# Attention and feed-forward on one core: VectorE's share of the exponentials chosen while scheduling, late groups added from another bank

## Chip, cores, metric

One core of a Trainium2 chip. The time is device time in microseconds (us), the median over executions; lower is better.

## The reference

```python
x = A_x                                             # [1, 2048, 512] bf16
g = sigmoid((x * gate_w).sum(-1, keepdims=True))
a = mha(x, wqkv, wo)                                # 32 heads of 16, softmax over 2048 keys
b = (silu(x @ w_gate) * (x @ w_up)) @ w_down        # 512 -> 1792 -> 512
return g * a + (1 - g) * b
```

Attention has 32 × 2048 × 2048 = 134 million exponentials. They are most of ScalarE's work: 841.0 of its 864.7 busy us.

## The kernel before

The work is cut into 32 units (four heads, 512 queries). A unit has 64 banks of scores, each 128 keys by 512 queries for one head. A bank goes one of two ways:

- two banks at a time through ScalarE (`s_t` to `e_t`, one exponential instruction of 128x1024);
- one bank at a time through VectorE (`d_t` to `y_t`): an eviction that scales the score so that its 16-bit pattern is nearly the exponential, and after four banks (a *block*) seven more steps of 128x2048 that correct it.

Either result is multiplied by V into `o_ps`, the only output bank. At the end of a unit `o_ps` is copied out. PSUM's eight banks are all taken: four for `s_t`, one each for `d_t` and `o_ps`, two (`m`) shared by projections and the feed-forward part.

The order of instructions is fixed while building by a small planner that keeps a reckoned time for TensorE, VectorE and ScalarE. Cut to what matters here:

```python
def on_vector(b):            # VectorE's banks: eight fixed places in each unit but the first
    return b % (4 * KT) in (0, 7, 14, 21, 32, 39, 46, 53) and 4 * KT <= b < 4 * (SLOTS - KT) + 24

def emit_pair(bs):           # two banks for ScalarE
    ...
    act(out=e_t[:], in_=s_t[:], func=ACT.Exp, scale=inv_sqrt_dh)
    plan.act = max(plan.act, plan.pe + 0.27) + 0.905

def first():                 # in emit_d: one bank for VectorE
    vec.tensor_scalar(out=y[:, i * QBW:(i + 1) * QBW], in0=d_t[:, :], scalar1=EXP_A, scalar2=EXP_B, ...)
    ...                      # after the fourth: seven steps are queued in vops, 0.73 or 1.26 us reckoned each;
                             # the last one appends the block to `late`
def pv(bs):                  # multiply by V; a unit's one output bank
    ...
    mm(o_of[un][32 * j:32 * j + 32, :], lhsT=vaug[...], rhs=e_of.pop(b), start=(i == 1), stop=(i == KT), ...)

def emit_pv():
    ...
    if complete(closed):     # only when all 64 banks, late blocks too, are in
        close(closed); closed += 1
```

## Time and profile before

| | before |
|---|---|
| time | 900.39 us (900.07 to 900.48, 4 runs) |
| ScalarE busy | 864.7 us, 96% |
| exponential instructions on ScalarE | 902 |
| VectorE busy; its blocks | 738.3 us, 82%; 61 |
| ScalarE's wait for scores | 10.9 us in 16 waits |
| TensorE's wait for ScalarE to free a score buffer | 74.6 us |

An engine that is busy for 96% of the span and waits for 10.9 us in it is the bound. How the lines show this is in the prediction below. One view also belongs here: the granted TensorE clock (PEclk, the column after the engines; 1.00 is the full clock) around ScalarE's longest gap, in steps of 3.4 us.

```profile
core 0: us, PE busy (x) PEld busy (x) DVE busy (x) ACT busy (x) POOL busy (x), PEclk, DMA share, GB/s
86.10:89.50 3.40, 3.40 (x11) 0.57 (x10) 2.63 (x3) 3.26 (x4) 0.00 (x0) 0.57 0.02 5
89.50:92.90 3.40, 1.55 (x13) 0.53 (x11) 2.18 (x4) 2.07 (x3) 0.00 (x0) 0.93 0.33 74
92.90:96.30 3.40, 3.40 (x18) 0.49 (x15) 3.16 (x5) 2.05 (x2) 0.00 (x0) 0.50 0.00 1
96.30:99.70 3.40, 3.40 (x25) 0.74 (x22) 0.81 (x2) 1.74 (x2) 0.00 (x0) 0.56 0.02 5
```

From 89.5 to 92.9 us TensorE is busy for only 1.55 of 3.4 us, since it waits for the late block and the copy. In the 6.8 us that follow it is granted about half its clock, and ScalarE is busy for 3.8 of them: to the gap of 2.33 us come two waits of 0.92 us. So the unit-end wait is paid twice here.

### The profile page before, as it was taken

The numbers are of one execution on the slowest core, as the hardware profiler recorded it, in microseconds if no ns is written. First come the engines' busy times: TensorE is split into PE (matmuls) and PEld (weight loads), VectorE is DVE, ScalarE is ACT, GpSimd is POOL, SyncE is SP. The second block draws the span as 40 slices with busy tenths as digits, with TensorE's granted clock in tenths as the row PEclk, the third lists the DMA queues.
The fourth block names the chain that finished last, engine by engine and source line by source line (L and its number), as shares of the span: only waits on it lengthen the run. The fifth ranks groups of instructions, "written<-read, shape, count | busy, mean of one in ns | idle before, by whom it ended". The sixth has DMA issues, their size and how long they took to land.

```text
span 899.6 us, 14223 instructions
## 1 busy us (share of the span) xinstructions
PE 800.7 (89%) x5168; PEld 207.8 (23%) x5168; DVE 738.3 (82%) x1032; ACT 864.7 (96%) x967; POOL 7.0 (1%) x29
## 2 busy tenths in 40 slices
PE   6999899999998899999889888989888889888886
PEld 2222222222222222222222222222222222222221
DVE  6379898998988889887878889978787988887784
ACT  3999899999999999999999999999999999999996
POOL 3000000000000000000000000000000000000000
PEclk9999899999999999999999999999999999999999
DMA  8301021121101112110001111100011121000000
GB/s 205 105 1 32 22 48 33 38 54 27 34 7 28 36 36 68 37 48 10 5 15 40 33 51 48 52 15 10 4 25 34 35 54 46 21 10 5 6 19 24
DMA packets 87534, 31.97 MB, mean 36 GB/s; under 512 B 75120, under 2 KB 87016, under 8 KB 87464
## 3 DMA queue, kind: packets, MB, share of 16 engines
q1 hardware_dynamic: 86408, 30.94, 14.0%
q8 instruction: 40, 0.66, 0.3%
q10 hardware_dynamic: 1056, 0.13, 0.1%
q14 instruction: 30, 0.25, 0.1%
HBM read 20.83 MB, written 2.34 MB: 26 GB/s over the span
## 4 chain that ended last, share of the span: by engine, by line
ACT 44%; PE 32%; issue 11%; DVE 10%; SPq 1%; DMA 1%; ACTq 0%; DVEq 0%
ACT e_t L161 41%; PE s_t L158 12%; PE o_ps L158 7%; DVE y_t L167 4%; DVE u_t L167 3%; ACT th L161 3%; PE gp L158 3%; PE d_t L158 2%; PE up L158 2%; PE dps L158 2%; PE kp L158 1%; PE a_ps L158 1%; SPq L174 1%; PE qp L158 1%; DVE mt L167 1%
## 5 line engine op out<-in xcount | busy, mean ns | idle before, releaser
L161 ACT ACTIVATE e_t<-s_t 128x1024 bf16<-128x1024 f32 x902 | 841.0, 1075 | 11.6 <-PE s_t L158 10.9
L158 PE MATMUL s_t<-qx,kaug 64*128 64x512 bf16 x1692 | 330.9, 385 | 74.3 <-ACT e_t L161 72.8
L167 DVE TENSOR_SCALAR y_t<-d_t 128x512 uint16<-128x512 f32 x244 | 167.7, 687 | 85.1 <-PE d_t L158 81.6
L158 PEld LDWEIGHTS <-kaug 64*128 64x128 bf16 x2048 | 101.6, 93 | 404.3 <-issue 397.7
L158 PE MATMUL o_ps<-e_t,vaug 128*32 128x512 bf16 x1804 | 172.5, 391 | 1.6 <-DVE osb L167 0.8
L167 DVE TENSOR_TENSOR u_t<-u_t,z_t 128x2048 f16<-128x2048 f16 x122 | 148.9, 1220 | 2.4
L158 PE MATMUL d_t<-qx,kaug 64*128 64x512 bf16 x228 | 85.7, 376 | 0.0
L167 DVE TENSOR_TENSOR y_t<-y_t,u_t 128x2048 uint16<-128x2048 uint16 x61 | 74.3, 1218 | 0.6
L158 PEld LDWEIGHTS <-vaug 128*32 128x32 bf16 x2048 | 44.1, 95 | 132.7 <-issue 129.0
L158 PE MATMUL gp<-xT,wg 128*128 128x512 bf16 x224 | 68.5, 388 | 0.0
L158 PE MATMUL dps<-wd_t,mt 128*128 128x512 bf16 x224 | 67.8, 384 | 0.0
L158 PE MATMUL up<-xT,wu 128*128 128x512 bf16 x224 | 67.1, 387 | 0.0
L167 DVE SCALAR_TENSOR_TENSOR gs<-th,gp 128x512 bf16<-128x512 bf16 x56 | 38.2, 681 | 15.2 <-ACT th L161 14.8
L167 DVE TENSOR_SCALAR u_t<-z_t 128x2048 f16<-128x2048 uint16 x61 | 42.2, 692 | 1.6
L167 DVE TENSOR_SCALAR z_t<-y_t 128x2048 uint16<-128x2048 uint16 x61 | 42.2, 691 | 1.6
L167 DVE TENSOR_SCALAR u_t<-u_t 128x2048 f16<-128x2048 f16 x61 | 41.9, 686 | 0.8
L167 DVE SCALAR_TENSOR_TENSOR mt<-gs,up 128x512 bf16<-128x512 bf16 x56 | 38.2, 682 | 5.0 <-PE up L158 4.0
L167 DVE TENSOR_SCALAR y_t<-y_t 128x2048 uint16<-128x2048 uint16 x61 | 41.7, 684 | 0.3
L161 ACT ACTIVATE th<-gp 128x512 bf16<-128x512 f32 x56 | 36.2, 647 | 0.0
L158 PE MATMUL o_ps<-y_t,vaug 128*32 128x512 bf16 x244 | 24.6, 390 | 4.8 <-DVE y_t L167 4.7
L167 DVE CAST osb<-o_ps 128x512 bf16<-128x512 f32 x32 | 21.9, 685 | 7.6 <-PE o_ps L158 7.4
L158 PEld LDWEIGHTS <-mt 128*128 128x128 bf16 x263 | 16.3, 99 | 45.9 <-issue 38.8
(97 smaller groups left out, 316.1 us busy)
## 6 DMA issues: line engine op xcount, KB each, us to landing
wg<-in_B_w_gate_dram SPq DMA_DIRECT2D x56, 128.0 KB
wu<-in_B_w_up_dram SPq DMA_DIRECT2D x56, 128.0 KB
on<-osb SPq DMA_DIRECT2D x120, 16.0 KB
rb<-rr SPq DMA_DIRECT2D x15, 128.0 KB
wd_t<-in_B_w_down_dram SPq DMA_DIRECT2D x1, 1792.0 KB
qx<-qst SPq DMA_DIRECT2D x112, 16.0 KB
out_dram<-o_t SPq DMA_DIRECT2D x12, 128.0 KB
kaug<-on SPq DMA_DIRECT2D x20, 64.0 KB
```

The lines of the kernel that those rows point to most:

```text
L158: ordered(nc.tensor.matmul(*args, **kw))
L161: ordered(nc.scalar.activation(*args, **kw))
L167: return lambda *a, **kw: ordered(f(*a, **kw))
L174: nc.sync.dma_start_transpose(out=xT[:, dc, :], in_=x[:, dc * P:(dc + 1) * P])
```

## The change

The intent is to give VectorE an exponential whenever the planner finds it free, not at fixed places, and to let a unit close without its late blocks. A block that is late (a *late group*) is multiplied into one of the two `m` banks. VectorE then adds that bank to the unit's copied output (`of`, fp32). A unit closes after its sixteenth row of four banks, late blocks or not (`last`). To make room, the kernel has 12 buffers of exponentials in place of 15, and three `y` buffers for two.

```diff
-    EB = 15
+    EB = 12
-    def on_vector(b):
-        return b % (4 * KT) in (0, 7, 14, 21, 32, 39, 46, 53) and 4 * KT <= b < 4 * (SLOTS - KT) + 24
+    vset = set()
 ...
     def pv(bs, last):
         un = bs[0] // (4 * KT)
+        extra = un < closed
+        if extra:
+            o = m_tile("x_ps")
 ...
+        if extra:
+            def add():
+                blocks[un] -= 1
+                vec.tensor_tensor(out=(of_of if blocks[un] else osbs)[un][:, :], in0=of_of[un][:, :], in1=o[:, :],
+                                  op=ALU.add)
+                m_free(plan.dve)
+                if not blocks[un]:
+                    finish(un)
+            later(0.6, add)
 ...
-        vec.tensor_copy(out=osb[:, :], in_=o_of.pop(un)[:, :])
+        if blocks.get(un):
+            of_of[un] = work.tile([P, QBW], F32, tag="of", name="of", bufs=1)
+        vec.tensor_copy(out=(of_of if blocks.get(un) else osbs)[un][:, :], in_=o_of.pop(un)[:, :])
 ...
-        if complete(closed):
+        if last:
             close(closed)
 ...
-        if ... 0.216 * mms + (0.1 if plan.mode != "F" else 0.0) > most:
+        if ... 0.226 * mms + (0.1 if plan.mode != "F" else 0.0) > most:
 ...
+    def to_vector():
+        un, at_ = divmod(nxt, 4 * KT)
+        if vcur:
+            if nxt % 4 in [b % 4 for b in vcur["b"]]:
+                return 0
+            return 2 if at_ >= 4 * KT - 4 * (NV - vcur["i"]) else 1
+        if not un or at_ > (50 if un < UNITS - 1 else 4) or y_live[0] >= 3 or sum(v[0] for v in vops) > 6:
+            return 0
+        return 1
```

More of the change, by code (lines that the diff above doesn't have):

```diff
@@ L648, in emit_d @@
             y_live[0] += 1
-            vcur["y"] = vex.tile([P, NV * QBW], U16, tag="y", name="y_t", bufs=2)
+            blocks[b // (4 * KT)] = blocks.get(b // (4 * KT), 0) + 1
+            vcur["y"] = vex.tile([P, NV * QBW], U16, tag="y", name="y_t", bufs=3)
             vcur["i"], vcur["b"] = 0, []
@@ L667, in first @@
             mine = list(block["b"])
-            assert sorted(m % 4 for m in mine) == list(range(4))
+            assert sorted(m % 4 for m in mine) == list(range(4)) and mine[0] // (4 * KT) == mine[-1] // (4 * KT)
             vops.extend([
@@ L711, with pv @@
     o_of = {}
-    pv_n = {}
+    begun = set()
+    of_of = {}
+    blocks = {}
+    closed = 0
     o_end = [0.0]
-    def pv(bs):
+    def pv(bs, last):
         un = bs[0] // (4 * KT)
-        if un not in o_of:
-            while un and un - 1 not in osbs:
-                pay()
-            plan.pe = max(plan.pe, o_end[0])
-            o_of[un] = ps_o.tile([P, QBW], F32, tag="o", name="o_ps")
+        extra = un < closed
+        if extra:
+            o = m_tile("x_ps")
+        else:
+            if un not in o_of:
+                while un and un - 1 not in osbs:
+                    pay()
+                plan.pe = max(plan.pe, o_end[0])
+                o_of[un] = ps_o.tile([P, QBW], F32, tag="o", name="o_ps")
+            o = o_of[un]
         for b in bs:
             n, j = b // 4, HEADS[b % 4]
-            i = pv_n[un, j] = pv_n.get((un, j), 0) + 1
+            first = extra or (un, j) not in begun
+            begun.add((un, j))
             c0 = (4 * UNIT[un][1] + j) * VC
@@ L728, in pv @@
                 force(v_chain[n])
-            mm(o_of[un][32 * j:32 * j + 32, :], lhsT=vaug[:, n % KT, c0:c0 + 32], rhs=e_of.pop(b),
-               start=(i == 1), stop=(i == KT), tile_position=(0, 32 * j), skip_group_check=True)
+            mm(o[32 * j:32 * j + 32, :], lhsT=vaug[:, n % KT, c0:c0 + 32], rhs=e_of.pop(b),
+               start=first, stop=extra or last, tile_position=(0, 32 * j), skip_group_check=True)
             e_left.pop(b, None)
         spend("C", 1, max(e_end.pop(b, 0.0) for b in bs))
-    def complete(un):
-        return all(pv_n.get((un, j)) == KT for j in range(4))
+        if extra:
[7 more added lines that the diff above has]
+            later(0.6, add)
     onc = {}
@@ L753, in post, with settle @@
         osbs[un] = osb
-        vec.tensor_copy(out=osb[:, :], in_=o_of.pop(un)[:, :])
+        if blocks.get(un):
+            of_of[un] = work.tile([P, QBW], F32, tag="of", name="of", bufs=1)
+        vec.tensor_copy(out=(of_of if blocks.get(un) else osbs)[un][:, :], in_=o_of.pop(un)[:, :])
+    def settle(un):
+        qb, g = UNIT[un]
+        osb = osbs[un]
         if g == 1:
@@ L957, with finish, part @@
     nb = 4 * SLOTS
-    a_banks = [b for b in range(nb) if not on_vector(b)]
-    pq = [a_banks[i:i + 2] for i in range(0, len(a_banks), 2)]
-    dq = [b for b in range(nb) if on_vector(b)]
+    nxt = 0
     done = 0
-    closed = 0
     here = {}
+    def finish(un):
+        settle(un)
+        qb, g = UNIT[un]
+        if qb < QB - 1 and g == G - 1:
+            recip(qb, G, plan.slot)
+        if qb == QB - 1 and g == G - 3:
+            recip(qb, G - 2, plan.slot)
+        if un == UNITS - 2:
+            here[un] = recip_here(osbs[un])
+            spend("F", 1, plan.dve + 0.2)
+            for i in range(TQ):
+                def part(cs=slice(i * P, (i + 1) * P)):
+                    recip16(here[un][1][:, cs], here[un][0][:, cs])
+                    vec.tensor_tensor(out=osbs[un][:, cs], in0=osbs[un][:, cs], in1=here[un][1][:, cs],
+                                      op=ALU.mult)
+                    if cs.stop == QBW:
+                        m_free(plan.dve)
+                later(1.2, part)
     def close(un):
@@ L968, in f @@
             o_end[0] = plan.dve + 0.1
-            qb, g = UNIT[un]
-            if qb < QB - 1 and g == G - 1:
-                recip(qb, G, plan.slot)
-            if qb == QB - 1 and g == G - 3:
-                recip(qb, G - 2, plan.slot)
-            if un == UNITS - 2:
-                here[un] = recip_here(osbs[un])
-                spend("F", 1, plan.dve + 0.2)
-                for i in range(TQ):
-                    def part(cs=slice(i * P, (i + 1) * P)):
-                        recip16(here[un][1][:, cs], here[un][0][:, cs])
-                        vec.tensor_tensor(out=osbs[un][:, cs], in0=osbs[un][:, cs], in1=here[un][1][:, cs],
-                                          op=ALU.mult)
-                        if cs.stop == QBW:
-                            m_free(plan.dve)
-                    later(1.2, part)
+            if not blocks.get(un):
+                finish(un)
         later(0.6, f)
     def pv_ready(now):
-        if late and late[0][1][0] // (4 * KT) == closed and (now is None or late[0][0] <= now):
-            return late[0][1]
+        if late and (now is None or late[0][0] <= now):
+            un = late[0][1][0] // (4 * KT)
+            if un == closed or un < closed and (now is None or m_ready() is not None and m_ready() <= now):
+                return late[0][1]
         if done < SLOTS and done // KT == closed and not (now is not None and done in v_chain
                                                           and not v_chain[done].done()):
-            bs = [b for b in range(4 * done, 4 * done + 4) if not on_vector(b)]
+            bs = [b for b in range(4 * done, 4 * done + 4) if b not in vset]
             if all(b in e_of for b in bs) and (now is None or max(e_end[b] for b in bs) <= now):
@@ L999, in pvs_ready @@
     def pvs_ready(now):
-        if pv_ready(now) is None:
-            return 0
-        if late and late[0][1][0] // (4 * KT) == closed and late[0][0] <= now:
-            n = done
-        else:
-            n = done + 1
-        if len(late) > 1 and late[1][0] <= now and late[1][1][0] // (4 * KT) == closed:
-            return 2
-        if n < SLOTS and n // KT == closed and not (n in v_chain and not v_chain[n].done()):
-            bs = [b for b in range(4 * n, 4 * n + 4) if not on_vector(b)]
-            if all(b in e_of for b in bs) and max(e_end[b] for b in bs) <= now:
-                return 2
-        return 1
+        k = n = 0
+        for ready, bs in late[:2]:
+            un = bs[0] // (4 * KT)
+            if ready <= now and (un == closed or un < closed and k == 0 and m_ready() is not None and m_ready() <= now):
+                k += 1
+        for n in (done, done + 1):
+            if n < SLOTS and n // KT == closed and not (n in v_chain and not v_chain[n].done()):
+                bs = [b for b in range(4 * n, 4 * n + 4) if b not in vset]
+                if all(b in e_of for b in bs) and max(e_end[b] for b in bs) <= now and (
+                        closed in o_of or (not closed or closed - 1 in osbs) and o_end[0] <= now):
+                    k += 1
+        return min(k, 2)
     def emit_pv():
@@ L1017, in emit_pv @@
         bs = pv_ready(None)
-        pv(bs)
-        if late and late[0][1] is bs:
+        is_late = late and late[0][1] is bs
+        last = not is_late and done % KT == KT - 1
+        pv(bs, last)
+        if is_late:
             late.pop(0)
             y_live[0] -= 1
+            if bs[0] // (4 * KT) == closed:
+                blocks[closed] -= 1
         else:
             done += 1
-        if complete(closed):
+        if last:
             close(closed)
@@ L1044, in side @@
         t = m_ready() if takes else 0.0
-        if t is None or t > plan.pe + 0.1 or 0.216 * mms + (0.1 if plan.mode != "F" else 0.0) > most:
+        if t is None or t > plan.pe + 0.1 or 0.226 * mms + (0.1 if plan.mode != "F" else 0.0) > most:
             return None
@@ L1054 @@
     SLACK = 0.2
-    while pq:
-        if pq[0][-1] // 4 > plan.slot:
+    def to_vector():
[7 more added lines that the diff above has]
+        return 1
+    while nxt < nb:
+        if min(nxt + 1, nb - 1) // 4 > plan.slot:
             begin(plan.slot + 1)
@@ L1068 @@
         if room > 0.02:
-            d_ok = (vcur or y_live[0] < 2) and dq and dq[0] <= pq[0][-1] + 2 and not d_wait and d_end[0] <= plan.pe + 0.05
-            if d_ok:
-                emit_d(dq.pop(0))
+            if to_vector() and not d_wait and d_end[0] <= plan.pe + 0.05:
+                vset.add(nxt)
+                emit_d(nxt)
+                nxt += 1
                 continue
@@ L1086 @@
                 continue
-        if dq and dq[0] + 6 <= pq[0][0]:
-            while not vcur and y_live[0] >= 2:
-                next_pv()
-            emit_d(dq.pop(0))
+        if to_vector() == 2:
+            vset.add(nxt)
+            emit_d(nxt)
+            nxt += 1
             continue
-        emit_pair(pq.pop(0))
-    while closed < UNITS:
+        emit_pair(list(range(nxt, min(nxt + 2, nb))))
+        nxt += 2
+    while closed < UNITS or late or vops:
         fill_dve()
@@ L1103 @@
         else:
-            while pv_ready(None) is None:
-                pay()
-            emit_pv()
+            next_pv()
     for c in sorted(pace.chains, key=lambda c: c.deadline):
@@ L1115 @@
         pay()
-    assert not vops and not late and not dq and not d_wait
+    assert not vops and not late and not vcur and not d_wait and nxt == nb
     assert not at
```

## The prediction

> **What bounds the kernel now.** I read the page first: busy share by engine, then the costliest groups.
>
> ```profile
> PE 800.7 (89%) x5168; PEld 207.8 (23%) x5168; DVE 738.3 (82%) x1032; ACT 864.7 (96%) x967; POOL 7.0 (1%) x29
> ...
> L161 ACT ACTIVATE e_t<-s_t 128x1024 bf16<-128x1024 f32 x902 | 841.0, 1075 | 11.6 <-PE s_t L158 10.9
> L158 PE MATMUL s_t<-qx,kaug 64*128 64x512 bf16 x1692 | 330.9, 385 | 74.3 <-ACT e_t L161 72.8
> L167 DVE TENSOR_SCALAR y_t<-d_t 128x512 uint16<-128x512 f32 x244 | 167.7, 687 | 85.1 <-PE d_t L158 81.6
> ```
>
> ScalarE is busy for 96% of the span. Its 902 exponentials of two score banks each waited only 11.6 us in all, while the score matmuls waited 74.3 us, nearly all of it for ScalarE to free a score buffer. VectorE makes the other exponentials, 244 banks in 61 blocks of four, and waits 81.6 us for TensorE to deliver them. So ScalarE is the bound; the other two engines have about 75 and 160 us to spare. The mean of 1075 ns counts overlap twice. The step comes from the timeline of ScalarE: 71 exponentials in one run of 65.32 us, 0.920 us each, and 22 in 20.32 us, 0.924. I use 0.923.
>
> Next, the same by stage, to see whether this holds everywhere:
>
> ```profile
> core 0: us, PE busy (x) PEld busy (x) DVE busy (x) ACT busy (x) POOL busy (x), PEclk, DMA share, GB/s
> 20.00:60.00 40.00, 36.66 (x216) 9.79 (x214) 18.48 (x28) 38.48 (x43) 0.00 (x0) 1.00 0.25 67
> 60.00:150.00 90.00, 84.64 (x555) 22.04 (x557) 81.64 (x116) 85.45 (x96) 0.00 (x0) 0.94 0.15 32
> 150.00:400.00 250.00, 232.02 (x1506) 59.88 (x1505) 218.82 (x300) 248.11 (x281) 0.00 (x0) 0.99 0.16 38
> 400.00:640.00 240.00, 215.64 (x1412) 54.70 (x1413) 198.54 (x266) 238.66 (x266) 0.00 (x0) 1.00 0.11 27
> 640.00:870.00 230.00, 200.12 (x1308) 51.14 (x1301) 189.95 (x257) 229.18 (x257) 0.00 (x0) 1.00 0.10 25
> ```
>
> From 150 us on ScalarE leaves about 4 us of 720 idle. Only the stage from 60 to 150 us, where the projections of keys and queries fall, has three engines near 91 to 95% and ScalarE idle for 4.5 us. The timeline there shows why:
>
> ```profile
> 90.82 0.69 DVE L167 TENSOR_SCALAR y_t<-y_t 128x2048 uint16<-128x2048 uint16 x1
> 91.56 0.40 PE L158 MATMUL o_ps<-y_t,vaug 128*32 128x512 bf16 x4 [1.06 <-DVE y_t L167]
> ...
> 92.01 0.69 DVE L167 CAST osb<-o_ps 128x512 bf16<-128x512 f32 x1 [0.50 <-PE o_ps L158]
> ...
> 92.76 0.62 PE L158 MATMUL o_ps<-e_t,vaug 128*32 128x512 bf16 x3 [0.79 <-DVE osb L167]
> ...
> 94.01 2.11 ACT L161 ACTIVATE e_t<-s_t 128x1024 bf16<-128x1024 f32 x2 [2.33 <-PE s_t L158]
> ```
>
> A unit (64 score banks) cannot close until its last VectorE block is done (90.82), multiplied by V (91.56) and copied out of the only output bank (92.01); TensorE stands still in between, and ScalarE runs dry for 2.33 us. This is the place that the second half of the change is about. It is rare: over the whole trace the output matmuls waited 4.7 us for late blocks, in 10 waits.
>
> **What the Trainium skill says.** "ScalarE: Activation LUTs", section "What ACT_TABLE_LOAD costs", gives 186 ns plus 0.833 ns per element with immediate operands, and about 93 ns of overlap back to back: 946 ns for 1024 elements. The trace's step of 920 ns is 3% less; I use the trace's. "VectorE: DVE Perf Modes", section "Why PSUM operands drop a tier", holds fp32 from PSUM to one element per cycle. The trace agrees: 512 elements from PSUM take 687 ns, as long as 2048 16-bit elements from SBUF (z_t<-y_t, 691 ns). So the new adds, which read a PSUM bank, will not be cheap. "TensorEngine Tiling (Array Packing)", section "Key Properties", says that changing the tiling mode drains TensorE. The timeline agrees: from a lone score matmul (d_t, 308.49) to the next output matmul (308.79) is 0.30 us, where a step in one mode is about 0.21, so a change costs some 0.09 us.
>
> **The change, part by part.** I counted instructions in the two built orders.
>
> ScalarE: 902 exponentials become 890; the share of VectorE goes from 61 to 67 blocks. The six extra blocks lie in units 8, 14, 17, 22, 26 and 29, all in the stretch where ScalarE is the bound, so the saving is on the path: 12 × 0.923 = 11.1 us.
>
> VectorE: a block is four evictions of 687 ns, four cheap steps of 692, 691, 686 and 684, and three products or sums of 1220, 1220 and 1218: 9.16 us. Six of them: 55.0 us. New are 31 adds of a late group (output bank copy plus the other bank). No such row exists yet; the nearest is kaug<-a_ps,gval,bblk, one PSUM and one SBUF operand, at 749 ns: 31 × 0.749 = 23.2 us, an estimate. The copies out of the output bank stay 32 (28 of them now to fp32; 685 ns assumed for both). Together +78.2 us. All rows of VectorE add up to about 772 us against 738.3 busy, since neighbours overlap, so I scale by 0.956: +75 us, 813 us busy, some 91% of the new span.
>
> TensorE: the number of matmuls is the same, 5168. But 12 pairs, which run side by side in the two row halves, become 24 single scores: 12 more steps of 0.21, 2.5 us. Mode changes go from 1543 to 1573: 30 × 0.09 = 2.7 us. Against 74.3 us of waiting for ScalarE, 5 us of TensorE are covered.
>
> Waits: the unit-end chain shown above goes away, as a late group now uses one of the two banks shared with the projections and the feed-forward part, and no longer holds the output bank. I put this at 3 us (the 2.33 us gap and a few tenths elsewhere). Fewer buffers for exponentials (12 for 15) should not matter then, as they bridged just this wait.
>
> Sum: 900.36 − 11.1 − 3 = 886.3, before anything that a fuller VectorE costs.
>
> **The rivals.** First, VectorE becomes the bound. For units 6 to 30 I multiplied the changed order by the rows' durations: VectorE 673 us, 644 after scaling; ScalarE needs 688 × 0.923 = 635 plus 48 tanh at about 0.48 = 658. (The tanh figure: from first to last exponential 870.5 us, less 11 idle, less 902 × 0.923, over 56.) That is 98%, against 85% before; in units 14 to 22 it is 235 against 234. Such a full engine is sometimes late, and there is one bank for VectorE's scores and there are two buffers for ScalarE's, so TensorE waiting 1 us for VectorE makes ScalarE wait too. For it: these ratios. Against it: the schedule reckons 0.73 and 1.26 us for steps that take 0.69 and 1.22, and 0.905 us for an exponential that takes 0.923, so on the chip VectorE will tend to be ahead of the order it was given. I expect some 4 us; if late VectorE work struck at each of the six fuller units and some of the others, 10 to 15 us, and the time would be 896 to 901.
>
> Second, the late groups take the shared bank from the projections, which need two in turn, and each add stands in front of other VectorE work. In the stage from 60 to 150 us nothing is gained (no exponential leaves it), while 4 to 5 adds come in where VectorE is at 91%. If it costs 1 us per late group in that stage and a few tenths later, it takes back 5 to 10 us: 892 to 897. For it: the three full engines there. Against it: the planner puts a late group down only when such a bank is free.
>
> Third, better than reckoned: all of ScalarE's 11.6 us of waits go away as well. That is the floor, 900.36 − 11.1 − 11.6 = 877.7, and unlikely, as 1.5 us lie before VectorE has any share, and another 1.5 us at 872 to 875 us, where a matmul of the last step needs a just finished unit.
>
> **Range and chances.** 886.3 plus 4 for VectorE's lateness gives 890. Down to 884 if that costs nothing and the first stage gets smoother; up to 898 if VectorE is late at most fuller units. Over 2% faster means below 882.4 us, which needs nearly all of ScalarE's waits gone: 6%. Over 2% slower means above 918.4 us, 30 us of new ScalarE idle time: 2%.
>
> **What would show it.** Right: 890 exponentials with a step still near 0.923; ScalarE busy near 854 us; its wait for scores between 8 and 18 us; VectorE near 813 us, its wait for d_t well below 81.6, near 30; score matmuls waiting for ScalarE 55 to 70 us; output matmuls waiting for VectorE's blocks or the copy near zero, none above 1 us. Wrong: ScalarE waits of over 20 us, with TensorE waiting for VectorE (scores for d_t, or the shared bank) just before; adds much dearer than 0.75 us; or a lower granted TensorE clock over a long stretch, which the order of instructions cannot tell.

## The result, and the profile after

The changed kernel takes **885.19 us** (884.99 to 886.99, 4 runs), 0.9836 of the time before, 95% interval 0.9819 to 0.9853. Ratios here are the mean time of one kernel's fast runs over that of the other's of the same rounds, so not quite the ratio of the medians that are quoted. The time lies inside the stated range (884 to 898), near its fast edge; 10.4 us less were forecast, and 15.2 us came.

The page of the changed kernel, busy shares and the rows that answer to those shown before; the last row is the new add:

```profile
PE 784.8 (89%) x5078; PEld 207.2 (23%) x5168; DVE 797.8 (90%) x1129; ACT 853.5 (97%) x955; POOL 7.0 (1%) x29
...
L160 ACT ACTIVATE e_t<-s_t 128x1024 bf16<-128x1024 f32 x890 | 830.3, 1080 | 7.0 <-PE s_t L157 6.0
L157 PE MATMUL s_t<-qx,kaug 64*128 64x512 bf16 x1668 | 333.3, 385 | 59.9 <-ACT e_t L160 55.8
L166 DVE TENSOR_SCALAR y_t<-d_t 128x512 uint16<-128x512 f32 x268 | 184.0, 687 | 28.0 <-PE d_t L157 25.1
...
L166 DVE TENSOR_TENSOR osb<-of,x_ps 128x512 bf16<-128x512 f32 x28 | 19.1, 681 | 2.8 <-PE x_ps L157 2.7
```

ScalarE is still the bound. It works 11.2 us less (864.7 to 853.5), and waits for scores 4.9 us less (10.9 to 6.0). With 0.5 us from an earlier first exponential (19.8 for 20.3 us) that is 16.6, against 16.3 by which the span fell (899.6 to 883.3). VectorE has 75.8 us less idle time (59.5 us more work in a span 16.3 us shorter); 56.5 us of it are its wait for scores, which went from 81.6 to 25.1 us. (TensorE's busy time is of 5078 matmul records, 90 are missing, so it isn't compared.)

By stage, the changed kernel:

```profile
core 0: us, PE busy (x) PEld busy (x) DVE busy (x) ACT busy (x) POOL busy (x), PEclk, DMA share, GB/s
60.00:150.00 90.00, 84.25 (x585) 23.65 (x593) 85.55 (x122) 90.00 (x103) 0.00 (x0) 1.00 0.15 33
...
400.00:640.00 240.00, 217.38 (x1403) 55.29 (x1421) 223.44 (x306) 237.98 (x267) 0.00 (x0) 1.00 0.10 27
```

The stage from 60 to 150 us gained most: ScalarE, idle there for 4.55 us before, is never idle, and the granted clock is 1.00 for 0.94. From 400 to 640 us ScalarE has slightly more idle time than before, 2.0 for 1.3 us. The longest wait of the changed kernel comes later, at 737 us, and looks like the first rival of the prediction:

```profile
734.81 0.39 PE L157 MATMUL d_t<-qx,kaug 64*128 64x512 bf16 x1
...
735.05 1.22 DVE L166 TENSOR_TENSOR u_t<-u_t,z_t 128x2048 f16<-128x2048 f16 x1
...
736.19 0.68 DVE L166 TENSOR_SCALAR y_t<-d_t 128x512 uint16<-128x512 f32 x1
736.79 0.74 DVE L166 SCALAR_TENSOR_TENSOR o_t<-a_ps,gval,bblk 128x512 bf16<-128x512 f32 x1
...
736.93 0.37 PE L157 MATMUL d_t<-qx,kaug 64*128 64x512 bf16 x1 [0.98 <-DVE y_t L166]
...
737.62 1.02 ACT L160 ACTIVATE e_t<-s_t 128x1024 bf16<-128x1024 f32 x1 [1.08 <-PE s_t L157]
```

VectorE evicts `d_t` late (736.19), since its order has a step of 1.22 us in front (735.05). TensorE, which wants to write the next bank there, stands for 0.98 us, and ScalarE runs dry for 1.08 us. Whether VectorE is late because it is full, or because of that order alone, e7 will tell.

### The profile page after: what moved, and what is told of

Read it like the earlier page. It is cut to its first block, busy times and chain, and to the rows that moved or that the text cites. A ratio compares the mean times of both kernels' runs of the same rounds, so it can differ in the third digit from the quotient of the medians.

```text
span 883.3 us, 14242 instructions
## 1 busy us (share of the span) xinstructions
PE 784.8 (89%) x5078; PEld 207.2 (23%) x5168; DVE 797.8 (90%) x1129; ACT 853.5 (97%) x955; POOL 7.0 (1%) x29
## 4 chain that ended last, share of the span: by engine, by line
ACT 40%; PE 29%; DVE 17%; issue 10%; SPq 1%; DMA 1%; DVEq 0%; ACTq 0%
ACT e_t L160 37%; PE s_t L157 11%; DVE y_t L166 7%; PE o_ps L157 6%; DVE u_t L166 5%; ACT th L160 3%; PE d_t L157 3%; PE dps L157 2%; PE gp L157 2%; PE qp L157 1%; PE up L157 1%; SPq L173 1%; DVE mt L166 1%; PE kp L157 1%; DVE gs L166 1%
## 5 line engine op out<-in xcount | busy, mean ns | idle before, releaser
L160 ACT ACTIVATE e_t<-s_t 128x1024 bf16<-128x1024 f32 x890 | 830.3, 1080 | 7.0 <-PE s_t L157 6.0
L166 DVE TENSOR_SCALAR y_t<-d_t 128x512 uint16<-128x512 f32 x268 | 184.0, 687 | 28.0 <-PE d_t L157 25.1
L166 DVE TENSOR_TENSOR u_t<-u_t,z_t 128x2048 f16<-128x2048 f16 x134 | 163.4, 1219 | 1.9
L157 PE MATMUL d_t<-qx,kaug 64*128 64x512 bf16 x252 | 95.0, 377 | 1.7 <-DVE y_t L166 1.3
L166 DVE TENSOR_TENSOR y_t<-y_t,u_t 128x2048 uint16<-128x2048 uint16 x67 | 81.6, 1218 | 0.8
L157 PE MATMUL dps<-wd_t,mt 128*128 128x512 bf16 x200 | 62.4, 384 | 3.3 <-issue 3.3
L157 PE MATMUL gp<-xT,wg 128*128 128x512 bf16 x196 | 61.6, 384 | 2.5 <-issue 2.5
L157 PE MATMUL up<-xT,wu 128*128 128x512 bf16 x210 | 62.4, 383 | 1.5 <-issue 1.4
L157 PE MATMUL s_t<-on,kaug 64*128 64x512 bf16 x112 | 22.0, 384 | 3.3 <-ACT e_t L160 3.2
L166 DVE TENSOR_TENSOR osb<-of,x_ps 128x512 bf16<-128x512 f32 x28 | 19.1, 681 | 2.8 <-PE x_ps L157 2.7
```

What stands on the lines that cost most here:

```text
L157: ordered(nc.tensor.matmul(*args, **kw))
L160: ordered(nc.scalar.activation(*args, **kw))
L166: return lambda *a, **kw: ordered(f(*a, **kw))
```

## The experiments

My theory after reading the two traces: the gain is 11 us of exponentials taken off ScalarE plus 4 to 5 us of unit-end waits. The rivals: the granted clock was higher by chance; the freely chosen places matter, not their number; VectorE is so full that it takes back part of the gain. Twelve kernels ran, each in three rounds against the kernel before on the same chip, whose medians were 899.33, 899.51 and 899.47 us in the three sets of four.

| run | ScalarE exponentials | blocks | late groups | median us | ratio to before (95%) | ScalarE's wait for scores |
|---|---|---|---|---|---|---|
| before | 902 | 61 | 0 | 900.39 | 1 | 10.9 |
| after | 890 | 67 | 31 | 885.19 | 0.9836 (0.9819 to 0.9853) | 6.0 |
| e1 late groups only | 902 | 61 | 20 | 894.28 | 0.9946 (0.9925 to 0.9966) | 5.8 |
| e2 share only | 880 | 72 | 0 | 974.31 | 1.0834 (1.0810 to 1.0857) | 95.9 |
| e3 two blocks a unit | 902 | 61 | 7 | 890.48 | 0.9911 (0.9886 to 0.9936) | 1.4 |
| e4 before, 12 buffers | 902 | 61 | 0 | 901.45 | 1.0026 (1.0007 to 1.0044) | 11.4 |
| e5 after again | 890 | 67 | 31 | 885.24 | 0.9836 (0.9816 to 0.9856) | 7.1 |
| e6 adds twice | 890 | 67 | 31 | 891.38 | 0.9908 (0.9888 to 0.9929) | 11.9 |
| e7 lighter blocks | 890 | 67 | 31 | 883.65 | 0.9820 (0.9802 to 0.9837) | 5.1 |
| e8 measured times | 886 | 69 | 29 | 880.84 | 0.9791 (0.9772 to 0.9810) | 4.2 |
| e9 share only, early | 902 | 61 | 0 | 896.42 | 0.9955 (0.9937 to 0.9973) | 7.9 |
| e10 more blocks | 882 | 71 | 31 | 920.09 | 1.0229 (1.0206 to 1.0252) | 45.0 |
| e11 fewer late groups | 890 | 67 | 18 | 887.49 | 0.9865 (0.9849 to 0.9882) | 7.4 |
| e12 old price | 892 | 66 | 31 | 882.00 | 0.9800 (0.9785 to 0.9816) | 3.3 |

All passed the comparison with the reference, e7 too, which leaves out a product: the comparison does not notice it.

### e1: late groups only

```diff
     def to_vector():
+        return 2 if nxt % (4 * KT) in (0, 7, 14, 21, 32, 39, 46, 53) and 4 * KT <= nxt < 4 * (SLOTS - KT) + 24 else 0
 ...        # and, where a bank is given to VectorE, the limit of three live y buffers
```

The 12 buffers of exponentials, the third `y` buffer and the constant of 0.226 stay as in the changed kernel, so e1 differs from the kernel before by these too.

> Only the second half of the change: VectorE's share as before (the same fixed banks, 61 blocks, 902 exponentials on ScalarE), but late groups go to another bank and are added (20 of them here). My theory, that the 15 us are 11 us of 12 exponentials less plus 4 to 5 us of unit-end waits gone: 895 to 897 us, ScalarE's wait for scores down from 11 to about 6 us, no gap of 2 us near 90 us. Rival 1, the gap near 90 us was the granted clock of that stretch (0.89) and went by itself: the gap stays when the clock is low, and the time is 899 to 900. Rival 2, the freedom to place late groups is most of the gain: 890 or less.

Measured: 894.28 us, 4.9 us under before by the ratio, and ScalarE's wait at 5.8 us. That is my theory's wait, and 0.7 us under its range of times. The gap near 90 us is gone (with its two followers it was 4.2 us), and the granted clock of the stage from 60 to 150 us is 1.00.

Rival 1 can be judged over all the runs. Every kernel that holds a unit open until its late block is in (before, e2, e4, e9) has a gap of 2.3 to 3.5 us that ends between 90 and 95 us; in it a stretch of 6.8 us of half clock begins, with two more waits of 0.66 to 0.92 us. None of those with late groups has one. So the gap, and the low clock that comes with it, go with the open unit and not with chance.

### e2: share only

```diff
-        extra = un < closed
+        extra = False
 ...
-        last = not is_late and done % KT == KT - 1
+        last = (done + (not is_late)) // KT > closed and blocks.get(closed, 0) == (1 if is_late else 0)
```

> Only the first half: VectorE's share chosen while scheduling, but a unit stays open until its last late block is added in its own bank, as before; no adds of 128x512 from another bank. The scheduler then places 72 blocks (880 exponentials on ScalarE, 22 fewer than before, 10 fewer than after). My theory: 22 x 0.923 = 20 us less work on ScalarE, but more unit-end waits, as blocks may end late in a unit: ScalarE waiting for scores 15 to 25 us, 885 to 892 us, no better than after. Rival: the unit-end wait was never worth more than the one gap of 2.3 us, and the late groups with their adds cost more than they bring: 878 to 882 us, faster than after.

Measured: 974.31 us, 8% slower than before with 22 fewer exponentials on ScalarE. Neither expectation is near. The chain of events at one unit's end in its timeline:

```profile
443.60 0.69 DVE L166 TENSOR_SCALAR y_t<-y_t 128x2048 uint16<-128x2048 uint16 x1
444.34 0.62 PE L157 MATMUL o_ps<-y_t,vaug 128*32 128x512 bf16 x4 [5.03 <-DVE y_t L166]
...
445.01 0.69 DVE L166 CAST osb<-o_ps 128x512 bf16<-128x512 f32 x1 [0.72 <-PE o_ps L157]
...
445.75 0.62 PE L157 MATMUL o_ps<-e_t,vaug 128*32 128x512 bf16 x4 [0.79 <-DVE osb L166]
...
447.01 1.94 ACT L160 ACTIVATE e_t<-s_t 128x1024 bf16<-128x1024 f32 x2 [6.44 <-PE s_t L157]
```

and the granted clock there, in stretches of 4 us:

```profile
core 0: us, PE busy (x) PEld busy (x) DVE busy (x) ACT busy (x) POOL busy (x), PEclk, DMA share, GB/s
440.00:444.00 4.00, 0.00 (x0) 0.00 (x0) 3.86 (x5) 0.57 (x1) 0.00 (x0) 0.98 0.07 16
444.00:448.00 4.00, 2.86 (x20) 0.68 (x23) 0.98 (x2) 0.99 (x2) 0.00 (x0) 0.50 0.03 9
448.00:452.00 4.00, 4.00 (x27) 0.93 (x22) 1.37 (x3) 2.71 (x4) 0.00 (x0) 0.67 0.04 12
```

A block that begins as late as bank 50 is finished by VectorE only after all other work of its unit. TensorE waits 5 us for it, loses half its clock for the next microseconds, and ScalarE loses 6.4 us. Over the span the output matmuls waited 50.8 us for blocks and 18.1 us for the copy. So with blocks that may begin as late as bank 50, the free choice of places cannot be had without the second half of the change (e9 tries early ones).

### e3: at most two blocks in a unit

```diff
-        if not un or at_ > (50 ...
+        if started.get(un, 0) >= 2 or not un or at_ > (50 ...
```

> The changed kernel with at most two blocks per unit, so 61 blocks and 902 exponentials as before, all else as in after (7 late groups are left). My theory: the six blocks' 12 exponentials are 11 us, so 885.2 + 11 = 896 us, ScalarE's wait for scores 5 to 8 us. Rival, the gain comes from the freely chosen places (when, not how many): 888 to 891 us.

Measured: 890.48 us, in the rival's range and 5.5 us under mine. With the same 902 exponentials as before, ScalarE waits for scores 1.4 us in the whole span, against 10.9 before, and the granted clock is full until the last microseconds. In the list of its waits (us in all, times, longest):

```profile
ACT e_t L160 <- PE s_t L157: 1.4, 4, 0.5
```

So where VectorE's banks go, with the late groups, is worth 8.0 us by the ratios (1 to 0.9911), and the six further blocks, with the 24 late groups that come with them, 6.7 us (to 0.9836), not 11. The 4.3 us between 11 and 6.7 are about what ScalarE's waits grew by (1.4 to 6.0).

### e4: the kernel before with 12 buffers

```diff
-    EB = 15
+    EB = 12
```

> The kernel before with 12 buffers of exponentials in place of 15, nothing else. My theory, that the three buffers bridged the wait at the end of a unit for its late block: more ScalarE waits, 2 to 6 us longer, 902 to 906 us. Rival, the buffers did not matter: 900 to 901 us.

Measured: 901.45 us, between my range and the rival's; as a difference 0.26% slower than before, 2.3 us, the low end of what I expected. The gap near 90 us is 3.5 us for 2.3, and the output matmuls wait more for blocks (7.6 for 4.7 us) and for the copy (3.9 for 0.8), but ScalarE's wait is 11.4 for 10.9 us: the buffers do bridge that wait, as the prediction had it, but they matter little in all, even without late groups.

### e5, e6, e7: the changed kernel with more and with less work for VectorE

The order of all instructions is that of the changed kernel. e6 makes each add twice; e7 leaves one product out of each block.

```diff
+                for _ in range(1):
+                    vec.tensor_tensor(out=osbs[un][:, :], in0=of_of[un][:, :], in1=o[:, :], op=ALU.add)      # e6
```
```diff
-                (1.26, lambda: vec.tensor_tensor(out=ua, in0=ua, in1=za, op=ALU.mult)),
+                (1.26, lambda: None),                                                                         # e7
```

> The changed kernel unaltered, as the neighbour of the next three on one chip: 885 us, 0.983 to 0.985 of the kernel before, ScalarE's wait for scores near 6 us.

> The changed kernel with each of the 31 adds of a late group made twice (same result, same order of all else, the scheduler not told): 31 x 0.68 = 21 us more work on VectorE, none on the others. My theory, that VectorE is nearly full and its lateness is why six more blocks bring 6 to 7 us and not 11: ScalarE's wait for scores grows from 6 to 12 to 20 us, 4 to 12 us slower than the changed kernel beside it (889 to 897 us). Rival, VectorE still has slack (its recorded 90%) and something else takes the rest of the gain: within 2 us of the changed kernel.

> The changed kernel with one of the three 1.22 us products left out of each of the 67 blocks, wrong in its result on purpose, order and all else as in after: 67 x 1.22 = 82 us less work on VectorE. My theory: VectorE is never late, ScalarE's wait for scores falls from 6 to 1 to 3 us, 3 to 5 us faster (880 to 882 us). Rival, the waits come from the order of TensorE's work or the granted clock: within 1.5 us of the changed kernel.

Measured: 885.24, 891.38 and 883.65 us. Twenty-one us more work cost 6.1 us, and ScalarE's wait rose from 7.1 to 11.9 us, as my theory had it. But 82 us less work brought 1.6 us and not 3 to 5 (the rival had up to 1.5), and of ScalarE's wait of 7.1 us, 5.1 us stayed. The 1.08 us gap shown above stayed as well, with the same length. In its trace, too, the 1.22 us step stands in front of the eviction: that gap comes from the order and not from a full VectorE. So VectorE is close to its limit, but being full explains only about 2 us of the waits in the changed kernel; the rest lies in the order that the planner chose.

### e8: the planner with the traces' times

```diff
-        plan.act = max(plan.act, plan.pe + 0.27) + 0.905
+        plan.act = max(plan.act, plan.pe + 0.27) + 0.923
 ...        # 0.73 -> 0.69 and 1.26 -> 1.22 for VectorE's seven steps
```

> The changed kernel with the scheduler's reckoned times set to the traces' (0.923 us for an exponential in place of 0.905, 0.69 and 1.22 us for VectorE's steps in place of 0.73 and 1.26): it then places 69 blocks, 886 exponentials on ScalarE and 29 late groups. ScalarE's work falls by 4 x 0.92 = 3.7 us. If the lateness of VectorE takes half of it as it did with the six blocks: 882 to 884 us. Rival, VectorE is past the point where it pays: 885 to 888 us.

Measured: 880.84 us, 2.1% under before (interval 1.9 to 2.3%) and better than both kernels. ScalarE's wait is 4.2 us with 69 blocks, VectorE is busy for 809.4 us (92%), and there is no stretch of half clock before its last microseconds. It is better than reckoned, as the schedule also has fewer waits.

### e9: share only, with blocks that begin early

```diff
         extra = False                                # as e2
-        if not un or at_ > (50 ...
+        if not un or at_ > (30 ...
```

> As the run that chose the share but held each unit open, except that no block may begin after bank 30 of a unit's 64: 61 blocks, 902 exponentials on ScalarE, no late groups and no adds. My theory, that the 8% loss of that run came from blocks that end after their unit (TensorE waiting for the block, then at half its clock): with early blocks ScalarE's wait for scores is 1 to 6 us and the time 890 to 895 us, near the run with two blocks a unit. Rival, choosing places while a unit is held open is bad in itself: over 905 us.

Measured: 896.42 us, just above my range and far below the rival's. ScalarE's wait is 7.9 us, where I had 1 to 6; of it 4.8 us are the gap at 90 us with the two 0.92 us waits after it. So e2's loss came from blocks that begin late: they, and the 11 blocks that the limit leaves out, are all that differs. With e3 beside it, the same number of blocks with 7 late groups is 0.44% faster.

### e10: more blocks

```diff
         # e8, and
-        if not un or at_ > (50 if un < UNITS - 1 else 4) or y_live[0] >= 3 or sum(v[0] for v in vops) > 6:
+        if not un or at_ > (58 if un < UNITS - 1 else 4) or y_live[0] >= 3 or sum(v[0] for v in vops) > 4.5:
```

> The changed kernel with the scheduler's times set to the traces', blocks let begin up to bank 58 of a unit, and a block begun only when under 4.5 us of VectorE steps are pending: 71 blocks, 882 exponentials on ScalarE, 31 late groups. ScalarE's work is 3.7 us under that of the run with measured times (880.8 us). If VectorE still keeps up: 877 to 879 us. If it is full now: 881 to 886 us, with ScalarE's wait for scores over 8 us.

Measured: 920.09 us, 39 us worse than e8 with two more blocks, and far outside both expectations. From the list of its waits, and the timeline before one of the longest:

```profile
ACT e_t L160 <- PE s_t L157: 45.0, 49, 4.6
PE d_t L157 <- DVE y_t L166: 22.1, 25, 1.5
...
264.44 0.38 PE L157 MATMUL d_t<-qx,kaug 64*128 64x512 bf16 x1
...
266.24 0.37 PE L157 MATMUL d_t<-qx,kaug 64*128 64x512 bf16 x1 [1.10 <-DVE y_t L166]
...
267.44 0.58 PE L157 MATMUL d_t<-qx,kaug 64*128 64x512 bf16 x1 [0.83 <-DVE y_t L166]
...
269.18 0.58 PE L157 MATMUL d_t<-qx,kaug 64*128 64x512 bf16 x1 [1.15 <-DVE y_t L166]
...
270.28 1.02 ACT L160 ACTIVATE e_t<-s_t 128x1024 bf16<-128x1024 f32 x1 [4.47 <-PE s_t L157]
```

Now TensorE waits 22.1 us for VectorE to evict `d_t` (1.3 us in the changed kernel), and ScalarE waits 45 us for TensorE. But it is not the number of blocks that the trace shows. VectorE's banks come four in a row here, through one bank, with no scores for ScalarE in between. `to_vector` forces this (it returns 2) when a block has begun so late in its unit that its other banks must follow at once. This trace has ten such runs of two to four banks, and no other kernel's trace here has one; the waits of ScalarE right after them are 23.9 of the 45.0 us. In the order that e10's code builds, each of the ten begins at bank 52 to 58 of its unit, past the changed kernel's limit of 50. VectorE is busy for 90% of the span, less than in e8 (92%). So the later limit goes with about half of ScalarE's waits; the bare number of 71 blocks was not tested.

### e11 and e12

```diff
         # e11: e8, and at_ > 44 in place of 50
```
```diff
-        if t is None or t > plan.pe + 0.1 or 0.226 * mms + ... > most:      # e12: after, and
+        if t is None or t > plan.pe + 0.1 or 0.216 * mms + ... > most:
```

> As the run with the scheduler's times set to the traces', but blocks begin at most at bank 44 of a unit: 67 blocks and 890 exponentials as in the changed kernel, 18 late groups in place of 31 (13 adds less, 9 us of VectorE's work). By ScalarE's work alone 885; if late groups cost waits of their own, 881 to 883 us; if they are free, 884 to 886 us.

> The changed kernel with the one reckoned time that the change raised (0.226 us for a feed-forward or projection matmul when the scheduler asks if one fits) put back to 0.216: 66 blocks, 892 exponentials. ScalarE has 1.8 us more work: 886 to 888 us. Rival, this constant is part of why ScalarE's waits fell: 889 to 893 us.

Measured: e11 887.49 us, above all that was expected, with ScalarE's wait at 7.4 us: 13 fewer late groups don't make a faster kernel. It has e8's times, too, and is 2.3 us slower than the changed kernel. e12 882.00 us, faster than the changed kernel with one block less; both expectations fail. ScalarE waits 3.3 us in place of 6 to 7. The constant that the change raised did not help. These two say how large the part of chance is: both turns of a planner constant gave another order, and some 3 us more or less. The split into parts under e3 is therefore good to some 3 us, not better.

## Why the prediction was right, point by point

**The bound and the exponentials.** Right: ScalarE stayed the bound, at 97%. The 11.1 us reckoned for 12 exponentials are 11.2 us of busy time.

**VectorE.** It was given 75 us more; it took 59.5 (738.3 to 797.8). The add took 0.681 us and not 0.749, which is 2 us, and the rows grew by 75.3 us (780.7 to 856.0; the prediction's sum of 772 for the kernel before is 9 us low). That the busy time grew by 59.5 only means that instructions overlap their neighbours more when VectorE is fuller: the ratio of busy time to rows, taken as 0.956, was 0.946 before and is 0.932 after. Its wait for scores, forecast near 30, is 25.1 us.

**TensorE.** The score matmuls wait for ScalarE 59.0 us in all, within the 55 to 70 forecast: its extra steps were covered.

**The unit-end wait.** This term was mis-sized. Forecast were 3 us ("the 2.33 us gap and a few tenths elsewhere"); late groups alone brought 4.9 us (e1). The prediction read the gap but not its echo, the two 0.92 us waits at half clock that follow it: together 4.2 us. In the trace before, 6.4 of ScalarE's 10.9 us of waits end in a stretch of half clock or within 1 us of its end (these 4.2 among them; the others, near 365 and 872 us, follow no unit-end wait that was shown); in the one with two blocks a unit there is no such stretch before the last microseconds, and almost no wait. The rest of the forecast for these waits was also off: output matmuls waiting for late blocks did not go to zero, but to 2.4 us, plus 2.3 us for the late groups themselves; none of these is longer than 0.6 us.

**The rivals.** VectorE's lateness was put at 4 us. Its own share is about 2 us (e7); with the planner's order it is 4.6 (ScalarE's wait in after against e3). So the sign and size were fair, if in part for another reason: the planner's order, and not only a full VectorE. e6 shows that the danger was near: 21 us more of VectorE's work cost 6.1 us. The second rival, late groups in the way of the projections, did not come: the late groups waited 2.8 us for the shared bank, in 4 waits, but the stage from 60 to 150 us got faster, not slower. ScalarE's wait, forecast at 8 to 18 us, is 6.0.

**In sum**: −11.1, −3 and +4 were forecast; in the profile −11.2 of work, −4.9 of waits with all effects of both signs, and −0.5 at the start. The net of the waits was forecast at +1 us. That is where the 5 us come from by which the forecast was too slow. That the time still fell inside the range, 1.2 us from its edge, is in part luck: e12, one planner constant away, lies outside it at 882.00.

**What stays open.** Why one order of nearly the same instructions gives ScalarE 3 us and another 7 us of waits was not settled beyond the one gap at 737 us. Nor was the half clock isolated: no run changed it alone.

## What to carry to other kernels

When one accumulator must wait for a slow producer, let the late part go to a bank of its own and add it later: alone it brought 0.5% here, and it made possible a free share with blocks that begin late, which without it cost 8% (with early blocks the free share alone brought 0.45%). When a planner fixes the order, read what it makes of a new limit before trusting it: letting blocks begin at bank 58 put up to four of VectorE's banks in a row, and with two more blocks than at 881 us the time was 920. The fastest kernel here has the trace's durations in the planner (e8), but so has a slower one (e11). When reading a gap on the bounding engine, look at the granted clock in the microseconds after it; the wait may be paid twice.

## What the Trainium skill lacked or had wrong

- "TensorE: Matmul & The Clock Gate", section "Part 1: The HAM clock gate (the "warmup" mystery)", has half clock "after ≥1 idle window (~3.4µs)". What it lacks is how idle: another passage of the page lets short idle times do, without a number. Here TensorE was busy for 1.8 to 2.4 of the 3.4 us before each of the four stretches of half clock between 80 and 880 us (trace before). The length agrees: these stretches are of 3.4 or 6.8 us.
- The same page doesn't say what this does to an engine that TensorE feeds: in the trace before, 6.4 of ScalarE's 10.9 us of waits for scores end in such a stretch or within 1 us of its end.
- "ScalarE: Activation LUTs", section "What ACT_TABLE_LOAD costs": its formula gives an estimate of 946 ns a step for 1024 elements, back to back; the runs show 920 to 924.
- "VectorE: DVE Perf Modes", section "Why PSUM operands drop a tier", holds for the new add (one fp32 operand in PSUM, 512 elements: 681 ns, like an eviction at 687), but no page says how busy VectorE can be before engines in lockstep with it suffer: here at 92% (e8) ScalarE waited 4.2 us for scores, and at 90% in another order (e10) 45.0 us.
